# Seven edits to an FFT and expert-routing kernel: weight loads, a shorter load chain, one plain transform, a new order

## The chip, the cores and the metric

The kernel runs on one core of one Trainium2 chip. The metric is the device time of one execution in microseconds (us), lower is better; several runs are taken and the median is named.

## The reference

x has 8 batches of 2496 rows of 256 numbers. Each batch goes through a real FFT along its rows, a complex 256x256 product with bias, a soft shrinkage, and the inverse FFT. All 19968 rows are then routed to 8 experts: pairs of row and expert are taken in falling order of their logit, a row goes to the first expert that still has room, each expert takes 2496 rows, and its rows pass a two-layer network.

```python
X = np.fft.rfft(x, axis=1)
Yr = Xr @ w_r - Xi @ w_i + b_r
Yi = Xr @ w_i + Xi @ w_r + b_i
Yr = sign(Yr) * max(abs(Yr) - 0.01, 0)
Yi = sign(Yi) * max(abs(Yi) - 0.01, 0)
y = np.fft.irfft(Yr + 1j * Yi, n=2496, axis=1)
...
logits = y @ w_gate
for idx in argsort(-logits.flatten()):
    tok, e = idx // 8, idx % 8
    if assigned[tok] >= 0 or counts[e] >= 2496: continue
    assigned[tok] = e; counts[e] += 1
out[assigned == e] = max(y @ w1[e], 0) @ w2[e]
```

## The kernel before, in words

**Transforms (to about 525 us).** The FFT of length 2496 is done as products with fixed matrices. Per batch, eleven units of two column groups pass the first transform (L1158): the piece of x, `xt` of 117 rows by 512, is split into a rounded high part (ACT's cast, L1041) and the rest (DVE's subtraction, L1044), and three matmuls, high by high matrix, low by high matrix, high by low matrix, stand for one full-precision product. L1161 writes the result to DRAM and a second load brings it back turned. Batch 0 alone turns it on the core: PE transposes against an identity matrix (`h_idn`, built on GpSimd, called POOL in the profile) at L1175. The second stage (L1198) follows, then the spectral product with w_r and w_i (`wt`, L1214 and L1222), which takes its operands split too (L1203 to L1208), then the shrinkage: L1227 on DVE, and then for the batches in `SOFT` L1229 on ACT and L1230 on DVE, for the others L1232 and L1233 on DVE. The third stage is L1243; its result goes through DRAM to the last transform (L1280 split, or L1273 in one full-precision matmul for the batches in `PLAIN5`, which is batch 7), and the logits come at L1303.

**Head of the program.** All loads of constants, weights, bias and the first pieces of x are issued by SP (SyncE). `chain` ties them into one order: batch 0's x, the second-stage matrix in parts (`FX`, L1067), the spectral weights (L1087), the four copies of the gate's weights (L1096), the two bias rows, spread over 128 partitions (L1082), the third-stage matrix (`GX`, L1070), and only then batch 1's first piece of x (L1121).

**Routing and experts (from about 370 us).** Each expert's threshold is found by counting rounds (L468 to L514: DVE compares and counts, PE adds over partitions, L478 and L508). Once an expert is full, its rows' numbers are put into a list and the expert's remaining rows are worked off, which the code calls a closing; there are eight. 512-row jobs of rows that are certain run earlier. A job gathers its rows by indirect DMA on POOL (L664), stores and loads them in blocks on SP (L671, L675) and transposes them (L688), runs the first layer (L717) and the second (L736, L737) on PE, and scatters the result (L749, POOL).

**A closing's weights.** Which expert closes is known only as a number that the core computed. `load` fetches w1[e] and w2[e] in two halves each by indirect DMA on POOL (L641): an index tile `wi` holds the row number of each partition. Early jobs, whose expert is known, use plain DMA on SP (L639). Each half is split like the transforms' operands, by ACT's cast (L650) and DVE's subtraction (L651), 512 elements at a time, and frees its raw buffer then. For a closing's w1 the halves are read as `p (g k t) -> p g k t`, every fourth word.

**What sets the order.** Every instruction is added to a planner (class `Plan`) with an estimated duration, a due position, the buffers that it reads and writes, and an optional slack. `run` simulates the engines with these costs and emits the instruction that can start first, within a margin by due position; the emission order is each engine's program order. The positions come from a table `Q` and numbers such as `P1X`, `SLACK` and `LATE`; other numbers there give another order in every part of the program.

Of the kernel before, what the change touches and what calls it, by code (L numbers as in the profile page):

```python
# [13 lines left out]
I32 = mybir.dt.int32  # L14
# [266 lines left out]
P1X = -9.511  # L281
LATE = dict(sp=1.71, raw=7.61, gather=2.51, scatter=6.24)
SLACK = dict(split=1.565, count=0.366, back=0.155, lists=0.715, os=1.464, hid=0, mm4=0.149, mm4l=1.175, tr=1.717, trl=3.296, gate=1.037, gatel=2.447)
IOTA = True
Q = dict(hV=0.075, hA=0, hT=0, hP=0.003, e0=44.525, e1=79.699, en=128.427, le=5.378, ge=20.658, c0=1025.722, cs=57.378, c1=1077.172, c1a=1050.482, n0=126.722, n2=109.33, ll=59.361, gs=61.594, gl=3.592, be=14.408, bl=79.116, xp=17.05, f0=8.927, p1=0.211, p1s=0.613, p57=4.061, p57s=3.032, p5=4.568, p56s=0.773, p5s=0.966, xl=3.381, xs=1.132, m2=0.126, m3=-1.213, zz=1.738, m4=0.206, l5=4.727, s5=-1.32, w5=1.063, t5=1.684, g5=-0.333, r0=10.696, gb=0.7, gw=0.71, lg=0.568, aa=0.354, ba=1.906, sc=4.867, k2=2.422, xw=1.628, xv=4.067, xv2=4.926, gl2=11.503)
SOFT = (2, 3, 4, 5, 6)
# [172 lines left out]
def count(K, H, pos, c, no, ag, cols, pk, junk, acc, eqs=[], nt=1):  # L459
# [7 lines left out]
    for k in range(n):  # L467
        v(cols + 59, p, lambda k=k: V.scalar_tensor_tensor(junk[k % 2].t[:, 0:cols], H.m[:, 0:cols], c.t[:, k // ng:k // ng + 1], ag(k % ng)[:, 0:cols], op0=OP.is_ge, op1=OP.mult, accum_out=acc.t[:, k:k + 1]),  # L468
          [H.b_m, c, H.b_AG] + eqs, [junk[k % 2], acc])
# [76 lines left out]
def lists(K, H, pos, pre, ps2, cols, nt, iota, bs, pk, jl, gi, o, top, parts, group=None):  # L546
# [21 lines left out]
    for a, b in parts:  # L568
        for t0 in range(a, b, per):
# [9 lines left out]
            for q in range(n):  # L579
                plan.add('A', .29 + cols / 1200, pos(), lambda q=q, t=t0 + q, pl3=pl3: A.activation(K.junk.t[:, 0:cols], pl3.t[:, q, 0:cols], AF.Sign, bias=bs.t[:, t:t + 1], accum_out=sg.t[:, k0 + t:k0 + t + 1]), [pl3, bs], [sg, d], slack=SLACK['lists'])  # L580
# [38 lines left out]
class Experts:  # L619

    def __init__(self, K, H, YD, YDb, w1, w2, out):
        self.K, self.H, self.YD, self.YDb, self.out = K, H, YD, YDb, out
        self.w = (w1, w2)
        self.rows = (w1.rearrange("e d f -> (e d) f"), w2.rearrange("e (r m) d -> (e r) (m d)", m=4))
        self.scat = []

    def load(self, pos, e=None, wi=None, block=False):

        K, plan, v = self.K, self.K.plan, self.K.v
        W1, W2 = [], []  # L630
        for k in range(2):
            for m in range(2):
# [4 lines left out]
                if e is not None:  # L637
                    src = self.w[k][e].rearrange("(m p) f -> p m f", m=2)[:, m] if not k else self.w[k][e].rearrange("(g m p) d -> p g m d", g=2, m=4)[:, m]
                    K.dma(p, lambda r=r, src=src, k=k: K.nc.sync.dma_start(r.t.rearrange("p (m d) -> p m d", m=4) if k else r.t, src), 524e3, [], [r], run=1024 if k else 4096)  # L639
                else:  # L640
                    K.ind(p, lambda r=r, k=k, m=m: K.P.indirect_dma_start(out=r.t, out_offset=None, in_=self.rows[k],  # L641
                                                                          in_offset=bass.IndirectOffsetOnAxis(ap=wi.t[:, (2 + m if block and not k else m):(2 + m if block and not k else m) + 1], axis=0)), 524e3, [wi], [r], run=4096, late=LATE['raw'])
# [146 lines left out]
class Router:  # L789
# [10 lines left out]
    def early(self, pos):  # L800
# [11 lines left out]
        for e in range(8):  # L812
# [33 lines left out]
    def closing(self, i, pos):  # L846
# [117 lines left out]
        wa, wb, wi = K.sb("wi", [128, 1]), K.sb("wi", [128, 1]), K.sb("wi", [128, 4], I32)  # L964
        v(1, pw, lambda: V.tensor_scalar(wa.t, wf.t, 7.0, 256.0, op0=OP.min, op1=OP.mult), [wf], [wa])
        v(1, pw, lambda: V.tensor_tensor(wb.t, wa.t, H.pc[:, 1:2], op=OP.add), [wa, H.b_pc], [wb])
# [26 lines left out]
PLAIN1, PLAIN5 = (), (7,)  # L993
# [5 lines left out]
def phase_a(K, H, x, w_r, w_i, b_r, b_i, w_gate, cD1, cF, cG, cD5, YD, LG, NB=B):  # L999
# [51 lines left out]
    df = sb("xh", [117, 120])  # L1051
# [27 lines left out]
    def load_weights(after):  # L1079
        Bbt = sb("s2h", [128, 2, 256])  # L1080
        for c, bv in enumerate((b_r, b_i)):
            wl.append(add_dma(-79, lambda c=c, bv=bv: nc.sync.dma_start(Bbt.t[:, c], bass.AP(tensor=bv.tensor, offset=bv.offset, ap=[[0, 128], [1, 256]])), 128e3, [], [Bbt], late=0))  # L1082
# [13 lines left out]
        for q in range(4): wl.append(add_dma(-79, lambda q=q: nc.sync.dma_start(wg[32 * q:32 * q + 32, :, 8 * q:8 * q + 8], w_gate.rearrange("(m c) e -> c m e", c=32)), 8e3, [], [Bwg], after=[z_], run=32, late=0))  # L1096
# [5 lines left out]
    def batch(b):  # L1102
# [24 lines left out]
        for u in range(NU):  # L1127
# [23 lines left out]
            h, l = [sb(k, [117, 2, 256], F32R) for k in ("xh", "xl")]  # L1151
            ps = psum("p1", [120, 2, 256])
            st = gates['s1st', b, u] = sb("s1st", [120, 2, 256])
            split(pos1(u) - Q['xs'], t, lambda t=t, r=r, k_=k_: t.t[0:k_, r:r + 2], (h, lambda h=h, k_=k_: h.t[0:k_]), (l, lambda l=l, k_=k_: l.t[0:k_]), 'A', 'V', 512)

            def mm(h=h, l=l, ps=ps, k_=k_, M=M):
                for i, (a, v) in enumerate(((0, h), (0, l), (1, h))):
# [408 lines left out]
```

## Time and profile before

| what | value |
|---|---|
| median of 3 runs | 1454.51 us (1452.92 to 1456.67) |
| the profiled execution's own time | 1458.17 us |
| its span from first to last instruction | 1456.4 us |
| mean granted TensorE clock | 0.995 of full |
| PE (matmul) busy | 1422.1 us, 98% |
| PEld (weight load) busy | 1200.7 us, 82% |
| DVE busy | 1119.2 us, 77% |
| ACT busy | 813.3 us, 56% |
| POOL busy | 473.3 us, 32% |

PE is TensorE's matmul side and PEld its weight loads, which overlap matmuls; DVE is VectorE, ACT ScalarE, POOL GpSimd, SP the engine that issues plain DMAs. Matmuls are pipelined and their ends are modelled, so a PE shown busy need not be at its peak. Idle time of an engine that nothing waits for costs nothing.

### The profile page before, as it was taken

To read this page: it belongs to the slowest core of one execution; us is meant where nothing else is said; L and a number is where in the kernel's file an instruction comes from. 1 tells how busy PE (TensorE), PEld (TensorE's weight loads), DVE (VectorE), ACT (ScalarE), POOL (GpSimd) and SP (SyncE) were. 2 spreads that over 40 slices of the span, in tenths; PEclk is the share of its full clock that TensorE was granted. 3 is DMA by queue.
4 is the path that set the end of the run, shared out by engine and by line. 5 is a ranking of instruction groups with operands and counts; after the bars stand their busy time and mean duration, and the time that the engine had idled before them with its cause. 6 is when DMAs were issued, how large, how long until landed. Compare 5 with 4: busy or idle time off the path is not lost.

```text
span 1456.4 us, 33431 instructions
## 1 busy us (share of the span) xinstructions
PE 1422.1 (98%) x9630; PEld 1200.7 (82%) x9630; DVE 1119.2 (77%) x3210; ACT 813.3 (56%) x1919; POOL 473.3 (32%) x442
## 2 busy tenths in 40 slices
PE   8999999999999999999999999999999999999997
PEld 6978888888887867888888878788888888888886
DVE  4879778877999986899999999987876564553432
ACT  4766887878778765446536364545444652442331
POOL 0012222222224234312534454546354435312112
PEclk9999999999999999999999999999999999999999
DMA  6588797888877676332743545544443344321000
GB/s 209 170 289 273 222 299 224 284 277 242 269 212 264 200 202 210 125 115 83 208 116 113 162 123 156 154 139 135 131 143 121 99 136 139 110 71 37 24 23 30
DMA packets 218596, 238.11 MB, mean 163 GB/s; under 512 B 96310, under 2 KB 180387, under 8 KB 218403
## 3 DMA queue, kind: packets, MB, share of 16 engines
q1 hardware_dynamic: 198433, 177.56, 40.2%
q0 software_dynamic: 19840, 58.22, 12.8%
q8 instruction: 78, 1.28, 0.4%
q14 instruction: 115, 0.94, 0.2%
q10 hardware_dynamic: 130, 0.11, 0.0%
HBM read 138.10 MB, written 97.71 MB: 162 GB/s over the span
## 4 chain that ended last, share of the span: by engine, by line
PE 79%; DVE 13%; DMA 3%; ACT 2%; issue 2%; SPq 0%; POOL 0%; POOLq 0%; DVEq 0%; ACTq 0%
PE b L717 23%; PE b L736 15%; PE b L737 8%; PE b L1214 6%; PE b L1243 4%; PE b L1198 3%; PE pt L717 3%; PE b L1222 3%; PE b L1158 3%; PE pt L736 3%; PE b L1280 2%; PE pt L737 1%; PE b L1303 1%; DMA xt<-in_x_dram 1%; DVE xTl L1207 1%
## 5 line engine op out<-in xcount | busy, mean ns | idle before, releaser
L1044 POOL TENSOR_TENSOR s2l<-s2c,s2h 120x512 fp32r<-120x512 f32 (+1 forms) x84 | 107.4, 1289 | 396.5 <-ACT s2h L1041 336.5
L1214 PE MATMUL b<-wt,xTh 128*128 128x256 f32 x640 | 125.1, 291 | 0.0
L749 POOL DMA_INDIRECT out_dram<-xTh,li x64 | 66.4, 1038 | 171.4 <-DVE xTh L746 112.8
L1214 PEld LDWEIGHTS b<-wt,xTh 128*128 128x128 f32 x640 | 100.4, 191 | 9.6 <-issue 3.6
L1214 PE MATMUL b<-wt,xTl 128*128 128x256 f32 x320 | 93.8, 293 | 6.0 <-DVE xTl L1207 5.7
L749 POOL DMA_INDIRECT out_dram<-xTl,li x64 | 67.3, 1051 | 95.6 <-DVE xTl L746 53.8
L1198 PEld LDWEIGHTS b<-FG,sh 128*128 128x128 f32 x640 | 85.4, 194 | 9.3 <-issue 2.3
L1198 PE MATMUL b<-FG,sh 128*128 128x128 f32 x640 | 91.3, 280 | 1.2 <-DVE sh L1179 1.2
L1243 PE MATMUL b<-y,FG 64*128 64x256 f32 x640 | 81.2, 390 | 0.5 <-DVE y L1233 0.5
L745 ACT COPY xTh<-b 128x256 f32<-128x256 f32 x61 | 22.8, 374 | 86.1 <-PE b L737 85.3
L1243 PEld LDWEIGHTS b<-y,FG 64*128 64x128 f32 x640 | 58.6, 186 | 14.8 <-issue 2.6
L1214 PEld LDWEIGHTS b<-wt,xTl 128*128 128x128 f32 x320 | 61.2, 191 | 11.4 <-DVE xTl L1207 10.6
L1158 PE MATMUL b<-xh,d 117*120 117x512 f32 (+1 forms) x154 | 64.3, 424 | 5.4 <-ACT xh L1041 5.4
L1293 DVE STREAM_TRANSPOSE yT<-b 128x512 f32<-128x512 f32 x87 | 61.5, 709 | 8.3 <-PE b L1273 4.5
L1044 DVE TENSOR_TENSOR xl<-xt,xh 117x512 fp32r<-117x512 f32 (+1 forms) x77 | 53.9, 707 | 16.6 <-ACT xh L1041 16.1
L1280 PE MATMUL b<-s2h,d 120*128 120x512 f32 (+1 forms) x168 | 66.4, 404 | 0.0
L1227 DVE TENSOR_TENSOR y<-b,sx 128x512 f32<-128x512 f32 x80 | 54.8, 685 | 15.0 <-ACT sx L1225 14.0
L1216 DVE TENSOR_TENSOR b<-b,bf 128x512 f32<-128x512 f32 x80 | 55.3, 692 | 12.5 <-PE b L1214 12.5
L580 ACT ACTIVATE ajunk<-b,h_bs 128x156 bf16<-128x156 f32 x122 | 47.7, 391 | 27.5 <-PE b L575 23.1
L1282 ACT COPY yst<-b 117x512 f32<-117x512 f32 (+2 forms) x95 | 52.2, 557 | 19.4 <-DVE yT L1293 12.6
L1222 PE MATMUL b<-wt,xTh 128*128 128x256 f32 x320 | 62.9, 288 | 0.0
L717 PE MATMUL b<-yT,sh 128*128 128x512 f32 (+1 forms) x170 | 61.3, 384 | 0.0
(1154 smaller groups left out, 4947.0 us busy)
## 6 DMA issues: line engine op xcount, KB each, us to landing
T<-s4st SPq DMA_DIRECT2D x80, 256.0 KB
s2c<-T SPq DMA_DIRECT2D x80, 240.0 KB
YD<-yst SPq DMA_DIRECT2D x80, 234.0 KB
xt<-in_x_dram SPq DMA_DIRECT2D x35, 512.0 KB
sh<-T SPq DMA_DIRECT2D x35, 512.0 KB
T<-s1st SPq DMA_DIRECT2D x70, 240.0 KB
xt<-in_moe_w_dram SPq DMA_DIRECT2D x32, 512.0 KB
yT<-XG SPq DMA_DIRECT2D x48, 64.0 KB
```

What stands on the lines that cost most here:

```text
L717: T.matmul(ps.t[:, 0:w], lhsT=W1[m].t[:, a, 128 * ft:128 * ft + 128], rhs=x_.t[:, 0:w], start=q + m == 0, stop=q + m == 3)
L736: T.matmul(ps.t, lhsT=hh.t[:, u:u + 128], rhs=W2[ft // 4].t[:, :, ft % 4], start=ft == 0, stop=False)
L737: T.matmul(ps.t[:, 0], lhsT=hl.t[:, u:u + 128], rhs=w_[0], start=False, stop=ft == 7)
L749: ins = P.indirect_dma_start(out=self.out, out_offset=bass.IndirectOffsetOnAxis(ap=oi.t[0:M, oo + t:oo + t + 1], axis=0), in_=o.t[0:M], in ...
L1044: lambda: eng.tensor_tensor(lb[1](), src(), hb[1](), op=OP.subtract), [srcb, hb[0]], [lb[0]], port=True)
L1158: T.matmul(ps.t[0:M], lhsT=d1[0:k_, a, 0:M], rhs=v.t[0:k_], start=i == 0, stop=i == 2)
L1198: T.matmul(ps.t[:, :, dt, i], lhsT=sh[k // 8].t[:, k % 8, 128 * dt:128 * dt + 128], rhs=at(Ft, k), start=True, stop=True)
L1214: T.matmul(pc.t[:, c], lhsT=a.t[:, 1 - c, dt], rhs=wt[2 - c].t[:, w, dt], start=dt == 0 and a is th and w == 0, stop=dt == 1 and a is tl)
L1222: T.matmul(pa.t, lhsT=a.t[:, 2, dt], rhs=wt[0].t[:, w, dt], start=dt == 0 and a is th and w == 0, stop=dt == 1 and a is tl)
L1243: T.matmul(ps4[i].t[:, r], lhsT=at(Gt, 2 * (p - 1 + r) + c)[h], rhs=zs[r].t[h, c], start=c == 0, stop=c == 1)
L1280: T.matmul(ps.t[:, gs_], lhsT=d5[0:k_, a], rhs=v.t[0:k_, gs_], start=i == 0, stop=i == 2)
L1293: yt.append(plan.add('V', TU, pos + Q['t5'], lambda yT=yT, ps=ps: V.transpose(yT.t.rearrange("p g m r -> p (g m r)"), ps.t.rearrange("p g ...
```

## The change

Seven edits, with the lines of the kernel after some ten higher:

1. A closing's second weights come by plain DMA from SP; its address is made from a register that SP loads from a new element of `wi` (written by one more DVE operation). The first weights stay with POOL's indirect DMA.
2. The first weights' halves are now read as straight runs of 512.
3. The two bias copies and the four gate copies are issued by POOL and are no longer part of SP's chain.
4. Batch 6's first transform is one full-precision matmul per unit, without the split; its matrix `df` gets a tile of its own (`d1f`).
5. Batch 7 joins `SOFT`.
6. The planner's costs of counting, scan, list and sign steps and of the third stage are changed.
7. `P1X`, `SLACK` and `Q` hold new numbers throughout.

```diff
@@ constants
-P1X = -9.511
+P1X = -8.849
...
-SOFT = (2, 3, 4, 5, 6)
+SOFT = (2, 3, 4, 5, 6, 7)
+PLAIN1, PLAIN5 = (6,), (7,)
...
@@ counting
-        v(cols + 59, p, lambda k=k: V.scalar_tensor_tensor(junk[k % 2].t[:, 0:cols], ...
+        v(155 + cols, p, lambda k=k: V.scalar_tensor_tensor(junk[k % 2].t[:, 0:cols], ...
...
@@ lists
-            v(2 * C, pos(), lambda gm=gm, pre=pre: V.tensor_tensor_scan(...
-            v(65 + C, pos(), lambda gm=gm, pre=pre, mk=mk, lim=lim: V.scalar_tensor_tensor(...
+            v(4.5 * C, pos(), lambda gm=gm, pre=pre: V.tensor_tensor_scan(...
+            v(225 + C, pos(), lambda gm=gm, pre=pre, mk=mk, lim=lim: V.scalar_tensor_tensor(...
...
@@ load (weights of a closing)
+                elif k:
+                    def ld(r=r, m=m, reg=reg):
+                        if not m: reg.append(K.nc.values_load(wi.t[0:1, 4:5], engines=[mybir.EngineType.SP], ...))
+                        K.nc.sync.dma_start(r.t.rearrange("p (m d) -> p m d", m=4), self.w[1][bass.ds(reg[0], 1)].rearrange("o (g m p) d -> p (o g) m d", g=2, m=4)[:, m])
+                    q = K.dma(p, ld, 524e3, [wi], [r], run=1024)
+                    if m: q.ords.add(last)
+                    last = q
                 else:
-                    K.ind(p, lambda r=r, k=k, m=m: K.P.indirect_dma_start(out=r.t, out_offset=None, in_=self.rows[k],
...
+                    c = (2 if block else 0) + m
+                    K.ind(p, lambda r=r, c=c: K.P.indirect_dma_start(out=r.t, out_offset=None, in_=self.rows, ...
...
-                    return (W.t[:, i - 1].rearrange("p (g t k) -> p g t k", g=2, t=4) if i else r.t.rearrange("p (g k t) -> p g t k" if e is None else "p (g t k) -> p g t k", g=2, t=4))[:, o]
+                    return (W.t[:, i - 1] if i else r.t)[:, 512 * o:512 * o + 512]
...
@@ load_weights
-            wl.append(add_dma(-79, lambda c=c, bv=bv: nc.sync.dma_start(Bbt.t[:, c], ...), 128e3, [], [Bbt], late=0))
+            add_dma(-60, lambda c=c, bv=bv: nc.gpsimd.dma_start(Bbt.t[:, c], ...), 128e3, [], [Bbt], 'P', late=0)
...
-        for q in range(4): wl.append(add_dma(-79, lambda q=q: nc.sync.dma_start(wg[32 * q:32 * q + 32, :, 8 * q:8 * q + 8], ...
+        for q in range(4): add_dma(-50, lambda q=q: nc.gpsimd.dma_start(wg[32 * q:32 * q + 32, :, 8 * q:8 * q + 8], ...
...
-            chain(head + FX[0:1] + wl[2:4] + wl[4:] + FX[1:2] + wl[0:2] + FX[2:3] + GX[0:1] + FX[3:] + GX[1:])
+            chain(head + FX[0:1] + wl + FX[1:3] + GX[0:1] + FX[3:] + GX[1:])
...
@@ first transform
+            if b in PLAIN1:
+                plan.add('T', .86, pos1(u), lambda t=t, r=r, ps=ps, k_=k_, M=M: T.matmul(ps.t[0:M], lhsT=df.t[0:k_, 0:M], rhs=t.t[0:k_, r:r + 2], start=True, stop=True), [t, df], [ps])
...
@@ a closing's index tile
-            g8, wf, wi = sb("g8", [128, 8]), sb("wi", [128, 1]), sb("wi", [128, 2], I32)
+            g8, wf, wi = sb("g8", [128, 8]), sb("wi", [128, 1]), sb("wi", [128, 8], I32)
+            v(1, pos(), lambda wf=wf, wi=wi: V.tensor_scalar(wi.t[:, 4:5], wf.t, 7.0, 0.0, op0=OP.min, op1=OP.max), [wf], [wi])
```

The order of instructions moves at three places that matter here.

**The head, on SP.** Before, from the spectral weights to batch 1's first piece of x (`FG` holds matrix parts, `s2h` the bias, `wg` the gate's weights):

```order
7 L1087 DMA y_171<-in_w_i_dram 128x2x256
8 L1096 DMA wg<-in_moe_w_gate_dram 32x8x8 x4
9 L1067 DMA FG_164<-cF 128x768
10 L1082 DMA s2h_183<-in_b_r_dram 128x256
11 L1082 DMA s2h_183<-in_b_i_dram 128x256
12 L1067 DMA FG_164<-cF 128x768
13 L1070 DMA FG_192<-cG 128x1024
14 L1067 DMA FG_194<-cF 128x512
15 L1070 DMA FG_192<-cG 128x1024
16 L1070 DMA FG_208<-cG 128x512
17 L1072 DMA yT_215<-cD 120x256
18 L1121 DMA xt_267<-in_x_dram 128x1024
```

and in the changed kernel, first SP and then POOL, which had the identity matrix (`h_idn`) as its first work:

```order
7 L1096 DMA y_173<-in_w_i_dram 128x2x256
8 L1076 DMA FG_165<-cF 128x768 x2
9 L1079 DMA FG_182<-cG 128x1024
10 L1076 DMA FG_184<-cF 128x512
11 L1079 DMA FG_182<-cG 128x1024
12 L1079 DMA FG_188<-cG 128x512
13 L1081 DMA yT_190<-cD 120x256
14 L1130 DMA xt_268<-in_x_dram 128x1024
```

```order
5 L1576 UNCONDITIONAL_BRANCH
6 L1091 DMA s2h_116<-in_b_r_dram 128x256
7 L1091 DMA s2h_116<-in_b_i_dram 128x256
8 L1105 DMA wg<-in_moe_w_gate_dram 32x8x8 x4
9 masks.py:197 MEMSET h_idn 128x128
10 masks.py:199 ISA
11 masks.py:199 AFFINE_SELECT h_idn<-h_idn 128x128
```

SP's row of the piece of x moves up by the six copies; POOL's identity now stands behind them.

**A closing's second weights, POOL and SP.** Before, POOL fetches them (`xt`, L641) among gathers (L664), with spacers between (L349):

```order
244 L664 DMA xl_11377<-YD,li_10583 128x256
245 L349 ISA x14
246 L641 DMA xt_11456<-in_moe_w_dram,wi_10301 128x1024
247 L349 ISA x14
248 L641 DMA xt_11489<-in_moe_w_dram,wi_10301 128x1024
```

In the changed kernel SP does, between its stores (`XG`, L680) and loads (L684) of blocks:

```order
539 L680 DMA XG_11149<-s2c_10883 128x2x256
540 L684 DMA ex_11300<-XG_11149 32x8x64 x4
541 L680 DMA XG_11390<-FG_11210 128x2x256
542 L644 TENSOR_LOAD wi_10260
543 L645 ISA
544 L645 DMA xt_11419<-in_moe_w_dram 128x4x256
545 L645 ISA
546 L645 DMA xt_11440<-in_moe_w_dram 128x4x256
547 L680 DMA XG_11468<-s4st_11284 128x2x256
548 L684 DMA s2c_11520<-XG_11390 32x8x64 x4
549 L680 DMA XG_11627<-xl_11403 128x2x256
550 L684 DMA FG_11634<-XG_11468 32x8x64 x4
```

The two loads of the second weights have left POOL and stand, behind a register load, ahead of three block loads (L684) on SP's queue.

**Batch 6's first transform, on PE.** Before, each unit has three matmuls of L1158:

```order
1484 L1198 MATMUL b_4519<-FG_164,sh_4340 128x2x64 x4
1485 L1158 MATMUL b_4531<-xh_4206,d_95 120x512
1486 L1158 MATMUL b_4531<-xl_4263,d_95 120x512
1487 L1158 MATMUL b_4531<-xh_4206,d_95 120x512
1488 L1280 MATMUL b_4540<-s2h_4452,d_96 128x512
```

and in the changed kernel one, straight from the piece of x:

```order
1390 L1211 MATMUL b_4303<-FG_184,sh_3490 128x2x64 x4
1391 L1293 MATMUL b_4318<-s2h_4261,d_96 128x512
1392 L1293 MATMUL b_4318<-s2l_4272,d_96 128x512
1393 L1293 MATMUL b_4318<-s2h_4261,d_96 128x512
1394 L1166 MATMUL b_4328<-xt_4115,d1f 120x512
1395 L1316 MATMUL b_4341<-yT_4052,wg 32x64
```

Eleven such units change from three matmuls to one.

## Rows read from the trace of the kernel before

**Rows 1.** Busy time by stretch: us, engines' busy us (x instructions), PE clock, DMA share, GB/s:

```profile
85.00:370.00 285.00, 282.36 (x2608) 247.30 (x2606) 228.70 (x403) 222.80 (x488) 68.17 (x53) 0.99 0.83 259
370.00:525.00 155.00, 145.85 (x1468) 123.89 (x1468) 150.11 (x420) 114.94 (x290) 48.34 (x41) 1.00 0.74 235
525.00:1075.00 550.00, 545.65 (x3086) 446.28 (x3085) 491.64 (x1771) 276.03 (x695) 236.81 (x225) 1.00 0.49 144
```

**Rows 2.** PE's waits: what waited, for whom, us in total, times, longest:

```profile
PE b L1214 <- DVE xTl L1207: 5.7, 10, 1.4
...
PE b L508 <- DVE ge L506: 3.4, 4, 1.0
```

**Rows 3.** Timeline of PE in the head: start us, us, what [idle before <-releaser]:

```profile
16.52 1.76 PE L1175 MATMUL b<-h_idn,sp 128*128 128x128 f32 x12 [0.55 <-DVE sp L1146]
...
24.00 0.28 PE L1214 MATMUL b<-wt,xTl 128*128 128x256 f32 x1
27.91 0.78 PE L1158 MATMUL b<-xh,d 117*120 117x512 f32 x1 [3.63 <-ACT xh L1041]
```

**Rows 4.** Timeline of ACT in the head:

```profile
27.24 1.14 ACT L1041 CAST xh<-xt 117x512 fp32r<-117x512 f32 x2 [4.52 <-DMA xt<-in_x_dram]
```

**Rows 5.** Busy time in stretches of 2 us, columns as in rows 1:

```profile
10.00:12.00 2.00, 2.00 (x20) 2.00 (x20) 0.79 (x3) 0.90 (x6) 0.00 (x0) 1.00 1.04 392
...
14.00:16.00 2.00, 1.97 (x18) 1.82 (x17) 1.75 (x5) 1.41 (x6) 0.00 (x0) 1.00 0.76 181
16.00:18.00 2.00, 1.43 (x11) 1.27 (x12) 1.66 (x6) 1.49 (x6) 0.00 (x0) 1.00 0.91 110
28.00:30.00 2.00, 2.00 (x4) 1.29 (x5) 2.00 (x4) 2.00 (x5) 0.00 (x0) 0.50 0.00 0
34.00:36.00 2.00, 2.00 (x17) 2.00 (x17) 1.23 (x3) 0.37 (x1) 0.00 (x0) 0.89 0.00 1
```

**Rows 6.** Timeline of SP's queue in the head, columns as in rows 3:

```profile
6.17 4.58 SPq L1096 DMA_DIRECT2D wg<-in_moe_w_gate_dram  x4
...
12.46 0.35 SPq L1082 DMA_DIRECT2D s2h<-in_b_r_dram  x1
...
17.83 0.53 SPq L1121 DMA_DIRECT2D xt<-in_x_dram  x1
```

**Rows 7.** The chain of work that ended last: start us, us, what:

```profile
27.91 3.22 PE b L1158 x6
...
55.97 1.40 PE b L1158 x6
...
539.43 1.79 PE b L1273 x4
```

**Rows 8.** Groups of ACT by form: out<-in xcount | busy us, mean ns | idle before:

```profile
L1041 ACT CAST xh<-xt 117x512 fp32r<-117x512 f32 x70 | 42.8, 626 | 5.3 <-DMA xt<-in_x_dram 5.2
...
L1229 ACT ACTIVATE y<-y,ml 128x512 f32<-128x512 f32 x50 | 36.2, 725 | 12.2 <-DVE y L1227 11.3 <-DVE g L527 0.5
```

**Rows 9.** Groups of DVE by form, columns as in rows 8:

```profile
L1044 DVE TENSOR_TENSOR xl<-xt,xh 117x512 fp32r<-117x512 f32 x70 | 49.2, 711 | 16.5 <-ACT xh L1041 16.1
...
L1232 DVE TENSOR_SCALAR y<-y 128x512 f32<-128x512 f32 x30 | 13.3, 442 | 0.3
```

**Rows 10.** Line L651, 695 to 1290 us: ns min/median/max; who waited (us, times):

```profile
L651 DVE TENSOR_TENSOR FG<-xt,FG x20: 674/682/722, 701.7 to 1287.8; 128x512 fp32r<-128x512 f32 x20
L651 DVE TENSOR_TENSOR sp<-xt,sp x16: 1045/1069/1090, 719.3 to 1183.2; 128x512 fp32r<-128x512 f32 x16
...
  POOL xt L641: 36.7, 6
```

**Rows 11.** Line L1532, near the program's end: a register load on SP's queue:

```profile
L1532 SPq TENSOR_LOAD <-h_fail x1: 492/492/492, 1331.0 to 1331.0; - x1
```

**Rows 12.** Timelines of SP and DVE around a closing's block: load issued, first use:

```profile
739.49 2.06 SPq L675 DMA_DIRECT2D xl<-XG  x4
...
743.95 0.44 DVE L688 STREAM_TRANSPOSE y<-yT 128x256 f32<-128x256 f32 x1
```

More of the change, by code (lines that the diff above doesn't have):

```diff
@@ L623, in __init__ @@
         self.w = (w1, w2)
-        self.rows = (w1.rearrange("e d f -> (e d) f"), w2.rearrange("e (r m) d -> (e r) (m d)", m=4))
+        self.rows = w1.rearrange("e d f -> (e d) f")
         self.scat = []
@@ L639, in load @@
                     K.dma(p, lambda r=r, src=src, k=k: K.nc.sync.dma_start(r.t.rearrange("p (m d) -> p m d", m=4) if k else r.t, src), 524e3, [], [r], run=1024 if k else 4096)
-                else:
-                    K.ind(p, lambda r=r, k=k, m=m: K.P.indirect_dma_start(out=r.t, out_offset=None, in_=self.rows[k],
-                                                                          in_offset=bass.IndirectOffsetOnAxis(ap=wi.t[:, (2 + m if block and not k else m):(2 + m if block and not k else m) + 1], axis=0)), 524e3, [wi], [r], run=4096, late=LATE['raw'])
+                elif k:
+                    def ld(r=r, m=m, reg=reg):
+                        if not m: reg.append(K.nc.values_load(wi.t[0:1, 4:5], engines=[mybir.EngineType.SP], min_val=0, max_val=7, skip_runtime_bounds_check_because="the number of an expert, held to at most 7 where it is written"))
+                        K.nc.sync.dma_start(r.t.rearrange("p (m d) -> p m d", m=4), self.w[1][bass.ds(reg[0], 1)].rearrange("o (g m p) d -> p (o g) m d", g=2, m=4)[:, m])
+                    q = K.dma(p, ld, 524e3, [wi], [r], run=1024)
+                    if m: q.ords.add(last)
+                    last = q
+                else:
+                    c = (2 if block else 0) + m
+                    K.ind(p, lambda r=r, c=c: K.P.indirect_dma_start(out=r.t, out_offset=None, in_=self.rows, in_offset=bass.IndirectOffsetOnAxis(ap=wi.t[:, c:c + 1], axis=0)), 524e3, [wi], [r], run=4096, late=LATE['raw'])
                 def part(i, o, k=k, r=r, W=W):
                     if k: return W.t[:, i - 1, 2 * o:2 * o + 2] if i else r.t.rearrange("p (m d) -> p m d", m=4)[:, 2 * o:2 * o + 2]
-                    return (W.t[:, i - 1].rearrange("p (g t k) -> p g t k", g=2, t=4) if i else r.t.rearrange("p (g k t) -> p g t k" if e is None else "p (g t k) -> p g t k", g=2, t=4))[:, o]
+                    return (W.t[:, i - 1] if i else r.t)[:, 512 * o:512 * o + 512]
                 for o in range(2):
@@ L1050, in phase_a @@
     add_dma(-100, lambda: A.dma_start(ds.t, cD1.rearrange("p (h m) -> p h m", h=2)), 112e3, [], [ds], 'A', run=960, k=13, late=0)
-    df = sb("xh", [117, 120])
+    df = K.one("d1f", [117, 120])
     plan.add('V', dve(120), -90, lambda: V.tensor_tensor(df.t, ds.t[:, 0], ds.t[:, 1], op=OP.add), [ds], [df])
@@ L1095, in load_weights @@
         z_ = plan.add('V', dve(256), -14, lambda: V.memset(wg, 0.0), [], [Bwg])
-        for q in range(4): wl.append(add_dma(-79, lambda q=q: nc.sync.dma_start(wg[32 * q:32 * q + 32, :, 8 * q:8 * q + 8], w_gate.rearrange("(m c) e -> c m e", c=32)), 8e3, [], [Bwg], after=[z_], run=32, late=0))
+        for q in range(4): add_dma(-50, lambda q=q: nc.gpsimd.dma_start(wg[32 * q:32 * q + 32, :, 8 * q:8 * q + 8], w_gate.rearrange("(m c) e -> c m e", c=32)), 8e3, [], [Bwg], 'P', after=[z_], run=32, late=0)
     CHUNKS = [(0, 2), (2, 4), (6, 4), (10, 4), (14, 4), (18, 4)], [(0, 4), (4, 4), (8, 4), (12, 4), (16, 4), (20, 2)]
@@ L1244, in batch @@
             gates['mm4', b, p] = [0]
-            gates['mm4', b, p][0] = plan.add('T', 2.12, pos + Q['m4'], mm4, zs + zd + [BG_[part(GQ, 2 * p)]], list(ps4), uses=[Gt[p // 8]], slack=SLACK['mm4l' if b == NB - 1 else 'mm4'])
+            gates['mm4', b, p][0] = plan.add('T', 1.95, pos + Q['m4'], mm4, zs + zd + [BG_[part(GQ, 2 * p)]], list(ps4), uses=[Gt[p // 8]], slack=SLACK['mm4l' if b == NB - 1 else 'mm4'])
             for i in range(2):
```

35 lines of the change are left out of this document (18 added, 17 removed).

## Prediction, made before the changed kernel had run

> **What bounds the kernel now.** I read the busy time by stage first, then the list of TensorE's waits, then the first 36 us in order of time. The windows [rows 1] show that TensorE (PE) is the engine that runs out of room in most of the program. From 525 to 1075 us, the early expert jobs and most routing rounds, it is busy 545.65 of 550 us; from 85 to 370 us, the transforms alone, 282.36 of 285 us. A busy PE is not a PE at its peak, so these are upper ends, but in those stretches only VectorE (DVE) comes near, with 491.64 us in the first of the two. From 370 to 525 us, where the last transforms and the first routing run together, DVE is the fullest: 150.11 of 155 us, while PE is down to 145.85. So a saving counts on PE everywhere, on DVE between 370 and 525 us, and elsewhere only where PE waits.
>
> The waits [rows 2] are few: matmuls of the spectral product on L1207 5.7 us, of the routing rounds on L506 3.4 us. The longest single one is of another line, in the head. PE's last matmul of batch 0's product starts at 24.00 us and the next, the first transform of batch 1, at 27.91 after 3.63 us of waiting [rows 3]; the cast on ScalarE (ACT) that it waits for had itself waited 4.52 us for its piece of x [rows 4], which SP issued only at 17.83 us [rows 6]. What follows is dearer than it looks: after that idle stretch the granted clock is 0.50, the lower of the two levels, at 28 to 30 us, and in the window from 34 it is still 0.89 [rows 5].
>
> **Early small loads to GpSimd's queue.** Two bias copies and four gate copies leave SP's chain. The gate's four alone occupy SP for 4.58 us from 6.17 [rows 6]. Their bytes do not vanish, and the DMA engines were not free: in the 4 us from 14 to 18 us, after the first bias copy went out at 12.46 [rows 6], they show a busy share of 0.76 and 0.91 while moving 181 and 110 GB/s, against 392 GB/s at 10 to 12 us [rows 5]. Lower end of what the piece of x gains: the idle share, 2 x (1 - 0.76) + 2 x (1 - 0.91) = 0.66 us. Upper end: those 4 us moved 582 KB, which at 392 GB/s takes 1.5 us, a gain of 2.5 us; and SP is no longer held either, which could give back the full 3.63 us of PE's wait. With the wait the low clock may go. Six matmuls of L1158 take 3.22 us at 27.91, and 1.40 us at full clock [rows 7]; the stretch from 28 to about 34 us is some 6 us at half clock, worth 3 us at most, less what DVE's chain would hold back anyway. So the head gives 0.7 to 6.6 us. I take 4.5, nearer the upper end, since the slow windows moved under half of what the engines can, and an early issue lets the slow packets share the engines with large ones: 2.4 us of the wait, and 2.1 for the clock. The identity matrix is now built on GpSimd behind the six copies; the transposes that use it come at 16.52 us [rows 3], and at the 4.58 / 4 = 1.15 us a copy that the gate's cost on SP it is ready by some 8 us, so I cost that at nothing.
>
> The Trainium skill has a rule against this edit ("DMA: Bandwidth & Descriptors", Issuing engines are not separate DMA queues): copies started from several engines end on the same 16 DMA engines, and only the time to initiate them is saved. By it the head would give about 0.7 us; the busy shares of 0.76 and 0.91 [rows 5] speak for it, the 4.58 us of issue [rows 6] against it.
>
> **Batch 6's first transform plain.** Each of 11 units loses one ACT cast (0.626 us [rows 8]) and one DVE subtraction (0.711 us [rows 9]): 6.9 us of ACT, 7.8 of DVE. PE gets one full-precision matmul for three: the last transform of batch 7 already runs so, and four such matmuls take 1.79 us, which is two units at 0.895 each, against 1.40 / 2 = 0.70 for a unit of three split ones [rows 7]. (The four records are the two passes of two units.) That is 11 x 0.195 = 2.1 us more on PE, before 525 us, where PE is 94 to 99% busy. The relief can only win back PE's waits on DVE there, at most some 2.0 of the 5.7 us. Between +2.1 and -2.0 I take 0.
>
> **Batch 7's shrinkage.** In ten pieces DVE loses the 0.442 us of L1232 [rows 9] (the operation behind it gives way to one of like kind and size), 4.4 us where DVE is full. ACT gets 0.725 us for each [rows 8], 7.3 us, and has 114.94 of 155 us taken [rows 1]. Against it, each piece's chain grows by 0.725 - 0.442 = 0.28 us, 3 us in ten. Between -4.4 and +3 I take -2.
>
> **Closing weights.** Plain rows of the first weights let the split read in a straight line. DVE's halves are 0.68 us where they read straight and 1.07 where they read every fourth word [rows 10]: 4 x 0.39 us a closing, 12 us in eight. PE is 99% busy beside it, so by itself this is worth nothing but margin for the routing rounds. GpSimd loses 16 loads and their spacers; SP gets 16 loads and eight register loads of 0.49 us [rows 11]. The loads move the same bytes in pieces of 1 KB instead of 4; the DMA engines' share there is 0.49 [rows 1], which leaves room. One more tiny operation a closing on DVE is under 0.44 us each. I cost all this at nothing; the cover is the lead that SP has with the blocks, and what happens without it is a rival below.
>
> **New plan.** The planner's cost of counting, scan and list steps is raised, and all constants of the order are new. What it can win is the 3.4 us of L506 waits [rows 2] and parts of the others; it can also put a matmul ahead of its input somewhere new, and I allow it as much as the waits of L1207 that it has to avoid again, less what is left of them: +4. I take -1, between -3.4 and +4.
>
> **Sum.** -4.5 + 0 - 2 + 0 - 1 = -7.5 us against this execution's own 1458.17 us (span 1456.4, 1.8 around it): 1450.7. The execution lies 3.7 above the median of 1454.51, so on the median **1447.0**. With every term at its best the sum is -16.4, at its worst +8.4: 1438 to 1463.
>
> **Rivals.**
> - *The DMA engines are the limit of the head.* Busy shares of 0.76 to 1.04 [rows 5] speak for it. x comes 0.66 us earlier, the 0.50 clock stays: -0.7 - 2 - 1 = -3.7, **1450.8**, at the edge of what can be measured. By the skill's rule on issuing engines this is the outcome. Chance 0.20.
> - *Batch 0 pays.* The bias copies now run beside batch 0's x. If the 2.5 us that they cost at 14 to 18 us move to the first microseconds, PE's first transforms start that much later and the head wins nothing: +2.5 - 2 - 1, about **1454**, no difference. Chance 0.10.
> - *SP is blocked by the second weights.* GpSimd waited 36.7 us in six waits for the split to free a raw buffer [rows 10], 6.1 us each. If such waits are now SP's, the gathered blocks' copies queue behind them; a block's load was issued 4.5 us ahead of its first use (739.49 to 743.95 [rows 12]). Where SP's wait exceeds 4.5 us the transposes come late, and with 1.6 us in each of eight closings PE loses 13 us: 1447 + 13 = **1460**. Against it: raw buffers come free sooner with the faster split. Chance 0.10.
> - *The plan closes the gaps too.* Head 6.6, shrinkage 4.4, L506 3.4, batch 6 2.0: -16.4, **1438.1**. Chance 0.12.
>
> **Chances.** The forecast's own case has 0.48 and reaches from 1441 to 1452. A measurement can tell about 0.3%, 4.4 us, from no change: faster is under 1450.1, slower over 1458.9. Faster: 0.43 of the forecast, 0.09 of the first rival, all 0.12 of the last, 0.64. Slower: the blocked SP and 0.02 of the batch 0 case, 0.12. The rest, 0.24, is no difference. The range 1438 to 1456 leaves out the blocked SP and the far tails of the others.
>
> **What would show it.** Right: SP issues batch 1's first piece of x well before 17.8 us; its cast waits under 2 us; the clock stays 1.00 from 24 to 36 us; the end of batch 0's and 1's work comes 4 to 5 us earlier. Batch 6's units show matmuls of about 0.45 us in pairs and no cast; PE's busy time before 525 us rises by about 2 us. Splits on DVE all read near 0.68 us. Wrong: x landing as late as before, or a 0.50 clock after it (first rival); gaps between PE's first matmuls of batch 0 (second); SP waiting on L651's successor while PE waits for the ffn's inputs (third). If the head gains as said and the end does not, the loss lies in the new order, and the stage where the shift shrinks names it.

## The result, and the profile after

The changed kernel takes 1439.99 us (median of 4 runs, 1439.27 to 1440.78), the kernel before 1453.78 (4 runs, 1452.92 to 1456.67): a ratio of **0.9901** on record, 95% interval 0.9887 to 0.9914, so 14.4 us less (12.5 to 16.4; the two medians alone differ by 13.8). The forecast was 1447.0, 7.5 us less than the 1454.51 known then: the right sign, about half the size, inside the range of 1438 to 1456 but outside the forecast's own case of 1441 to 1452.

The execution of the changed kernel that was profiled took 1440.23 us, about its median; the one of before took 1458.17, 4.4 us over this section's median. So of the 18 us between the two spans (1456.4 and 1438.4) some 4 are no effect of the change. Counted by PE's matmuls of the experts' first layer (1920 in each kernel), the 120th starts at 592.0 us before and 581.0 after, the 1120th at 1078.9 and 1062.6: 11.0 us of the 18 lie ahead of the 120th, 5.2 between the two and 1.7 behind.

Busy time by stretch, in the columns of [rows 1]:

```profile
85.00:370.00 285.00, 282.62 (x2601) 245.87 (x2601) 225.70 (x397) 215.92 (x477) 66.59 (x53) 0.99 0.82 258
370.00:525.00 155.00, 152.17 (x1556) 130.28 (x1554) 147.58 (x424) 126.70 (x319) 52.58 (x46) 1.00 0.78 248
525.00:1075.00 550.00, 549.66 (x3082) 452.08 (x3082) 488.74 (x1827) 268.90 (x688) 228.20 (x219) 1.00 0.49 143
```

PE's idle time fell from 9.15 to 2.83 us between 370 and 525 us, and from 4.35 to 0.34 between 525 and 1075; from 85 to 370 us it is as it was (2.64 and 2.38). These are stretches of time, and by the last of them the changed kernel is some 11 us further on in its program; counted from the 120th to the 1120th matmul, PE's idle time is 4.35 us before and 0.00 after. PE's waits, in the columns of [rows 2]:

```profile
PE b L1227 <- DVE xTl L1220: 3.0, 6, 0.7
PE b L1211 <- DMA sh<-T: 2.4, 1, 2.4
PE b L1146 <- DMA sh<-in_x_dram: 1.4, 1, 1.4
```

The spectral product's waits on VectorE (5.7 us on what was L1207) are 3.0, the routing rounds' 3.4 us on L506 are gone from the list, and two waits for DMAs are new; one of them, L1146, is batch 0's first transform waiting for x.

The head, in the timelines of PE, ACT and SP (columns as in [rows 3]). PE:

```profile
9.81 7.65 PE L1146 MATMUL b<-d1f,sh 117*128 117x120 f32 x64 [1.43 <-DMA sh<-in_x_dram]
18.24 1.76 PE L1188 MATMUL b<-h_idn,sp 128*128 128x128 f32 x12 [0.78 <-DVE sp L1155]
...
26.64 0.49 PE L1171 MATMUL b<-xh,d 117*120 117x512 f32 x1 [0.64 <-ACT xh L1050]
```

ACT:

```profile
25.97 1.14 ACT L1050 CAST xh<-xt 117x512 fp32r<-117x512 f32 x2 [1.80 <-DMA xt<-in_x_dram]
```

SP:

```profile
16.63 0.35 SPq L1130 DMA_DIRECT2D xt<-in_x_dram  x1
```

and the clock, in windows, first one of the kernel before and then two of the changed kernel:

```profile
30.00:40.00 10.00, 9.99 (x66) 9.51 (x65) 6.83 (x14) 5.41 (x13) 0.00 (x0) 0.78 0.20 51
```

```profile
28.00:30.00 2.00, 2.00 (x15) 1.84 (x14) 1.85 (x4) 2.00 (x6) 0.00 (x0) 1.00 0.00 0
30.00:40.00 10.00, 9.66 (x83) 9.19 (x83) 9.32 (x20) 4.54 (x12) 0.00 (x0) 1.00 0.18 51
```

Batch 0's transposes come 1.7 us later than before (18.24 against 16.52 in [rows 3]), batch 1's first transform only 1.3 us earlier (26.64 against 27.91). But PE's idle stretch ahead of it is 0.64 us instead of 3.63, and the granted clock stays at 1.00 where it was 0.50 from 28 to 30 us [rows 5] and 0.78 from 30 to 40.

### The profile page after: what moved, and what is told of

The parts are those of the page before. It is cut to its first block, busy times and chain, and to the rows that moved or that the text cites. A ratio compares the mean times of both kernels' runs of the same rounds, so it can differ in the third digit from the quotient of the medians.

```text
span 1438.4 us, 33189 instructions
## 1 busy us (share of the span) xinstructions
PE 1414.4 (98%) x9619; PEld 1195.2 (83%) x9619; DVE 1090.1 (76%) x3197; ACT 799.2 (56%) x1918; POOL 457.5 (32%) x432
## 3 DMA queue, kind: packets, MB, share of 16 engines
q1 hardware_dynamic: 205505, 185.65, 42.3%
## 4 chain that ended last, share of the span: by engine, by line
PE 89%; DVE 4%; DMA 3%; ACT 2%; issue 1%; SPq 0%; POOL 0%; POOLq 0%; DVEq 0%; ACTq 0%
PE b L726 27%; PE b L745 17%; PE b L746 8%; PE b L1227 7%; PE b L1256 4%; PE b L1211 4%; PE pt L726 4%; PE b L1235 3%; PE pt L745 3%; PE b L1293 3%; PE b L1171 2%; PE pt L746 2%; PE b L1316 1%; PE b L748 1%; DMA xt<-in_x_dram 1%
## 5 line engine op out<-in xcount | busy, mean ns | idle before, releaser
L754 ACT COPY xTl<-b 128x256 f32<-128x256 f32 x69 | 25.8, 374 | 78.4 <-PE b L746 69.7
L755 DVE TENSOR_TENSOR xTl<-b,xTl 128x256 f32<-128x256 f32 x69 | 28.9, 419 | 46.7 <-ACT xTl L754 46.6
L1295 ACT COPY yst<-b 117x512 f32<-117x512 f32 (+1 forms) x93 | 51.4, 562 | 17.2 <-DVE yT L1306 8.1
L1053 DVE TENSOR_TENSOR xl<-xt,xh 117x512 fp32r<-117x512 f32 (+1 forms) x66 | 49.6, 763 | 12.5 <-ACT xh L1050 9.5
```

What stands on the lines that cost most here:

```text
L1053: lambda: eng.tensor_tensor(lb[1](), src(), hb[1](), op=OP.subtract), [srcb, hb[0]], [lb[0]], port=True)
```

## The experiments

Each part was added to the kernel before by itself, and taken out of the changed kernel by itself. The runs were made in groups. The kernel before took 1454 us beside the runs of the first two parts, the first three with a moved due position and the one under "Relief or order", and 1458 to 1459 beside the others, so only ratios to the kernel before are compared. A thousandth is 1.45 us; each ratio's interval is some 1 to 1.5 thousandths either way, so a difference between two ratios is known to about 2 to 3 us.

| part | alone in the kernel before | taken out of the changed kernel (0.9901) |
|---|---|---|
| new numbers | 1.0015 (1.0006 to 1.0023) | 0.9922 (0.9911 to 0.9934) |
| batch 7 in SOFT | 1.0020 (1.0010 to 1.0029) | 0.9914 (0.9901 to 0.9927) |
| batch 6 plain | 0.9960 (0.9945 to 0.9976) | 0.9907 (0.9891 to 0.9923) |
| these three together | 0.9953 (0.9939 to 0.9967) | not run |
| small loads on GpSimd | 0.9990 (0.9981 to 0.9999) | 0.9916 (0.9901 to 0.9931) |
| closings' weights | 0.9953 (0.9940 to 0.9966) | 0.9950 (0.9937 to 0.9964) |

### The new numbers

```diff
-P1X = -9.511
+P1X = -8.849
...
-        v(cols + 59, p, lambda k=k: ...
+        v(155 + cols, p, lambda k=k: ...
```

(and `SLACK`, `Q` and the other costs; the second run has the reverse edit in the changed kernel)

> The kernel before with the change's numbers alone: P1X, SLACK, Q and the planner's costs. Theory A (the new order itself brings what came beyond the head): 6 to 10 us off, about 1446, most of it gained between 370 and 1075 us, with the waits of L508 on L506 (3.4 us before) gone. Theory B (the relief of VectorE by batch 7's shrinkage and batch 6's plain transform brings it, and the numbers only fit the order to that): within 2 us of before, about 1454, since the work on VectorE between 370 and 525 us is as before.

> The changed kernel with the old numbers (P1X, SLACK, Q, costs). Theory A: 6 to 10 us slower than the changed kernel, 1446 to 1450. Theory B: 0 to 3 us slower, 1440 to 1443.

Alone the numbers make the kernel before 2.2 us slower, against theory A and just outside theory B's 2 us; without them the changed kernel loses 3.1 us, less than theory A said, about theory B's upper end. The new order is not where the gain comes from, though it fits the changed kernel better than the old one. In the run with old numbers the 120th to the 1120th matmul of the first layer (counted in PE's timeline) take 480.7 us, in the changed kernel 481.6 and in the kernel before 486.8: the gain of the expert part is there without the new numbers.

### Batch 7's shrinkage

```diff
-SOFT = (2, 3, 4, 5, 6, 7)
+SOFT = (2, 3, 4, 5, 6)
```

(in the changed kernel; the other run has the reverse edit in the kernel before)

> The changed kernel with batch 7's shrinkage as before (SOFT without 7). Theory B: 4 to 9 us slower than the changed kernel, 1444 to 1449, lost between 370 and 525 us where VectorE is then full again. Theory A: at most 2 us slower, 1440 to 1442.

> The kernel before with batch 7 in SOFT alone. Theory B: 3 to 8 us off, 1446 to 1451. Theory A: within 2 us of before, 1452 to 1456. The prediction's own term was -2 us.

1.9 us lost in the changed kernel, with an interval that overlaps that kernel's own, and 2.9 us slower when added alone. Theory B fails in both; the second result lies a little outside theory A's 2 us too.

### The small loads

```diff
-            add_dma(-60, lambda c=c, bv=bv: nc.gpsimd.dma_start(...), ..., 'P', late=0)
+            wl.append(add_dma(-79, lambda c=c, bv=bv: nc.sync.dma_start(...), ..., late=0))
...
-            chain(head + FX[0:1] + wl + FX[1:3] + GX[0:1] + FX[3:] + GX[1:])
+            chain(head + FX[0:1] + wl[2:4] + wl[4:] + FX[1:2] + wl[0:2] + FX[2:3] + GX[0:1] + FX[3:] + GX[1:])
```

(and the gate's copies; the other run has the reverse edit in the kernel before)

> The kernel before with the bias and gate copies on GpSimd's queue and the shorter chain alone. Theory C (the head brings about 3.5 us, by the granted clock that stays up from 20 to 40 us): 3 to 5 us off, about 1450, clock 1.00 from 28 to 36 us although batch 0's first matmuls come some 1.5 us later. Theory D (the first transforms after the head absorb it, since they wait for DVE and DMA anyway): within 1.5 us of before.

> The changed kernel with the six small loads back in SP's chain. Theory C: 3 to 5 us slower than the changed kernel, 1443 to 1445, with the 0.50 clock back at 28 to 30 us. Theory D: within 1.5 us of it.

1.5 us gained in one direction, 2.2 lost in the other. The clock does what theory C says: windows of the changed kernel with the loads back on SP show the 0.50 again,

```profile
28.00:30.00 2.00, 2.00 (x5) 1.22 (x6) 2.00 (x4) 2.00 (x6) 0.00 (x0) 0.50 0.00 0
30.00:40.00 10.00, 9.66 (x70) 9.25 (x69) 7.16 (x15) 5.27 (x13) 0.00 (x0) 0.87 0.19 51
```

and its last transposes of batch 0 start at 46.5 us against 43.6 in the changed kernel. In the medians less than that 2.9 us is left of it: 1.5 us is theory D's edge, 2.2 lies between the two theories.

Two things make this part easier to read in the traces than in the medians. PE's order of instructions is the same with and without this edit, in both kernels, so no new order is mixed into it. And the run with the loads back on SP can be set beside the two other variants of the changed kernel run with it (the next section's first two, which keep the new head and PE's order as far as this): its 120th matmul of the first layer starts at 589.6 us, theirs at 585.5 and 585.9. In these single executions 3.7 to 4.1 us of the head's gain are still there when the expert part begins.

### The closings' weights

First the straight read alone is taken back: the first weights' split reads every fourth word again (`p (g k t) -> p g t k`; the words on `load` ahead of the prediction have the last two letters exchanged). To fit that, the second weights' loads on SP fetch four neighbouring rows per partition, in pieces of 4 KB instead of 1. In the two traces the compute engines run the same instructions in the same order as in the changed kernel.

```diff
-K.nc.sync.dma_start(r.t.rearrange("p (m d) -> p m d", m=4), self.w[1][bass.ds(reg[0], 1)].rearrange("o (g m p) d -> p (o g) m d", g=2, m=4)[:, m])
+K.nc.sync.dma_start(r.t, self.w[1][bass.ds(reg[0], 1)].rearrange("o (g p m) d -> p (o g) (m d)", g=2, m=4)[:, m])
...
-                    return (W.t[:, i - 1] if i else r.t)[:, 512 * o:512 * o + 512]
+                    return (W.t[:, i - 1].rearrange("p (g t k) -> p g t k", g=2, t=4) if i else r.t.rearrange("p (g k t) -> p g t k" if e is None else ...))[:, o]
```

> The changed kernel with the second weights still by plain DMA on SP, but laid out as before (four rows to a partition), so that the first weights' split reads every fourth word again; the order of instructions on every engine is the same. Theory E (the straight split brings the gain of the expert part, 6 to 8 us from 590 to 1080 us): 5 to 8 us slower than the changed kernel, 1445 to 1448, with waits of the routing rounds' matmuls on VectorE back. Theory F (taking the second weights off GpSimd brings it): within 2 us, 1439 to 1442. The prediction's term for both was nothing.

0.9934 (0.9920 to 0.9947), 4.8 us more than the changed kernel. Line L660 is the split's subtraction; in the changed kernel its groups read (columns as in [rows 10])

```profile
L660 DVE TENSOR_TENSOR sp<-xt,sp x32: 646/684/830, 438.5 to 1164.9; 128x512 fp32r<-128x512 f32 x32
...
  POOL xt L651: 2.8, 2
```

and in the run with the strided read

```profile
L660 DVE TENSOR_TENSOR sp<-xt,sp x32: 640/935/1093, 440.3 to 1174.7; 128x512 fp32r<-128x512 f32 x32
```

(the last line is the same there; half of the 32 belong to early jobs and read straight in both runs, the closings' 16 take 1.05 to 1.09 us), with these waits of PE from 525 to 1100 us, and this window:

```profile
PE b L509 <- DVE ge L507: 2.3, 4, 0.9
PE b L1286 <- DMA s2c<-T: 1.6, 1, 1.6
```

```profile
525.00:1075.00 550.00, 545.88 (x3046) 446.83 (x3045) 489.88 (x1813) 275.18 (x682) 228.09 (x218) 1.00 0.48 143
```

Of the 3.4 us that the routing rounds waited in [rows 2], 2.3 are back (on L509, which is L508 of the kernel before), and PE's idle time is 4.1 us again where the changed kernel has 0.34. L1286's wait for a transform's load is not the split's: two other runs that keep the straight read and PE's order (the loads back on SP, and the loads held back, below) have 1.3 us on it. Since PE's order is unchanged, each of its instructions can be compared with itself: from 560 us to 1009 us this run falls behind the changed kernel by 3.7 us more; 3.3 of that come in five steps of 0.4 to 1.0 us, all at a matmul of L509, between 714 and 988 us. The stretch from the 120th to the 1120th matmul takes 485.2 us instead of 481.6. So with the same program order and one slower read on ACT and DVE the routing rounds' chain is late again: theory E, a little under its lower end of 5 us. That the larger pieces of the second weights have a part in this is not excluded by a run of its own, but L509 waits for DVE, and GpSimd's waits for raw buffers are the same 2.8 us. Which of the two engines' relief counts, DVE's or ACT's, was not separated.

Then all of the closings' part, taken out and added alone (the diff is the one shown ahead of the prediction, under `load`):

> The changed kernel with the closings' weights as before: second ones by indirect DMA on GpSimd, strided split. Theories E and F: 6 to 9 us slower, 1446 to 1449. If the prediction's zero was right: within 2 us.

> The kernel before with the closings' weights alone as in the change (second weights by plain DMA on SP, straight split). Theory E (the straight split takes VectorE and ScalarE time out of the routing rounds, whatever the order): 4 to 8 us off, ratio 0.9945 to 0.997, and the stretch from the 120th to the 1120th matmul of the first layer, 486.8 us before, comes to 481 to 483. Theory G (it pays only with the new order): ratio over 0.998.

7.1 us lost, 6.8 us gained: the one part that gives the same in both directions, the largest of all. The stretch from the 120th to the 1120th matmul takes 481.1 us in the kernel before with this part alone, and 486.1 in the changed kernel without it. Over all twenty kernels of this document it takes 480.5 to 481.6 us in the nine that read the first weights straight and 485.2 to 486.8 in the eleven that do not, whatever their numbers, `SOFT`, batch 6, small loads or due position: a new order is no rival for these 5 us. Of the 7.1 us the straight read has 4.8; for the other 2.3 the intervals of the two runs overlap, and that they come from the second weights' way by SP is not shown. GpSimd's wait for a raw buffer, 36.7 us in [rows 10], is 2.8 in both runs above.

That wait did not vanish. It is SP's now, as the rival with the blocked SP had it. SP's queue in the changed kernel, 695 to 1300 us (what waited, for whom, us in total, times, longest):

```profile
SPq L645 <- DVE sp L660: 26.8, 5, 18.9
...
SPq L645 <- DVE sh L660: 15.5, 1, 15.5
```

That is 42.3 us in six waits for the split to free a raw buffer, two of them far over the 4.5 us from which the rival counted a loss. Its premise came, its price did not: the list of PE's waits between 695 and 1300 us of the changed kernel is empty. The register loads cost 0.27 us each. What covers the waits was not tried.

### Batch 6's plain transform, and the three together

```diff
-PLAIN1, PLAIN5 = (), (7,)
+PLAIN1, PLAIN5 = (6,), (7,)
```

(in the kernel before, with the new branch and the matrix's own tile; then the reverse in the changed kernel; then this with SOFT and the new numbers in the kernel before)

> The kernel before with batch 6's first transform plain alone. Theory H (PE pays 2 us and the relief is hidden, the prediction's term): between 2 us off and 2 us on, ratio 0.9985 to 1.0015. Theory I (the relief of ScalarE and VectorE lets the transforms run ahead): 3 to 6 us off, ratio 0.996 to 0.998.

> The changed kernel with batch 6's first transform split again. Theory H: ratio to the kernel before 0.989 to 0.9915 (the changed kernel's own is 0.9901). Theory I: 0.993 to 0.995.

> The kernel before with the new numbers, batch 6 plain and batch 7 in SOFT, so all of the change but the small loads and the closings' weights. Theory J (these three fit each other: alone the numbers and SOFT each cost 2 us, together they give 4 to 6 us between the end of batch 6 and the first jobs): ratio 0.996 to 0.9975. Theory K (the parts add up, and the gain is the closings' weights and the head): ratio over 0.999.

Alone the plain transform gives 5.8 us (theory I), taken out it costs 0.9 (theory H). The three together give 6.8 us, though two of them cost time alone: theory J, a little over its upper end. PE's own price was forecast rightly; two records are one unit, 0.86 us in the chain (0.895 was taken):

```profile
308.44 0.86 PE b L1166 x2
```

### What another order does

Most edits above also make another order, since the planner starts from new costs and dependencies (the strided read makes none, and the small loads none on PE). To see what that alone does, one due position was moved by a tenth.

```diff
-Q = dict(..., p1=0.211, ...)
+Q = dict(..., p1=0.311, ...)
```

(0.111 in the second run; 0.31 and 0.11 in place of 0.21 in the changed kernel)

> The kernel before with the due position of the first transforms of batches 2 to 7 moved from 0.211 to 0.311, nothing else: the planner makes another order. Theory L (orders differ by luck, as much as the single parts of the change do): ratio off 1 by 0.002 or more in at least one of this run and the next. Theory M (the order matters little): both within 0.0015 of 1.

> The same, moved to 0.111. Theories L and M as for the other shift.

> The changed kernel with the same due position moved from 0.21 to 0.31. Theory N (its numbers are the best of many orders, so another one loses): ratio to before 0.992 to 0.995 against the changed kernel's 0.9901. Theory M: 0.989 to 0.9915.

> The changed kernel with the due position of the first transforms moved from 0.21 to 0.11. Theory N (numbers that are the best of many orders): ratio to before 0.992 to 0.996. Theory M: 0.989 to 0.9915.

| | 0.1 later | 0.1 earlier |
|---|---|---|
| kernel before | 1.0015 (1.0006 to 1.0024) | 0.9978 (0.9970 to 0.9987) |
| changed kernel (0.9901) | 0.9946 (0.9933 to 0.9959) | 0.9930 (0.9917 to 0.9944) |

The kernel before gets 2.2 us slower by the one and 3.2 us faster by the other, the changed kernel slower by both, 6.5 and 4.2 us. So theory L holds, and theory N (with two neighbours each, no more). Then a part that moves the time by 2 or 3 us through the planner can't be told from a new order by one run, which holds for SOFT and for the numbers; and the changed kernel's own order is better than both of its neighbours by as much as a whole part of the change.

### Relief or order, for the plain transform

The kernel before with batch 6's matmul plain, but its casts and subtractions still made and their results unused:

```diff
-            if b not in PLAIN1: h, l = [sb(k, [117, 2, 256], F32R) for k in ("xh", "xl")]
+            h, l = [sb(k, [117, 2, 256], F32R) for k in ("xh", "xl")]
...
-            if b not in PLAIN1: split(pos1(u) - Q['xs'], t, ...
+            split(pos1(u) - Q['xs'], t, ...
```

> The kernel before with batch 6's first transform as one full-precision matmul, but with the 11 casts on ScalarE and 11 subtractions on VectorE still made, their results unused. With the split left out the ratio was 0.996. Theory I (relief of ScalarE and VectorE is the gain): back to 0.999 to 1.002. Theory O (the gain is not the relief, but PE no longer waiting for the split, or the order): 0.995 to 0.998.

0.9984 (0.9974 to 0.9993), between what the two theories allow, and nearer to 1 than the 0.9960. Some 3.5 us of the 5.8 go with the relief of ACT and DVE, if the order has no part in it; by the scatter above it may have as much. This stays open.

### Small loads held back

The changed kernel with a tiny GpSimd copy, which needs the fifth of batch 0's pieces of x, ahead of the six small loads:

```diff
+        gt = plan.add('P', .1, -61, lambda: P.tensor_copy(Bbt.t[:, 0, 0:2], gate.t[:, 0, 0:2]), [gate], [Bbt])
...
-            ..., 128e3, [], [Bbt], 'P', late=0)
+            ..., 128e3, [], [Bbt], 'P', after=[gt], late=0)
```

> The changed kernel with one tiny GpSimd copy ahead of the six small loads that needs the fifth piece of batch 0's x, so that they start only when it is in. Theory P (the small loads took batch 0's DMA time): the last turn of batch 0's first half comes about 1.5 us earlier than in the changed kernel, and the end 1 to 2 us earlier, ratio 0.988 to 0.9895. Theory Q (batch 0 is late for another reason, or batch 1's piece of x gets later by as much): 0.9895 to 0.992.

0.9909 (0.9894 to 0.9924), the changed kernel's own time. Its head, PE and then ACT and SP:

```profile
15.54 1.76 PE L1189 MATMUL b<-h_idn,sp 128*128 128x128 f32 x12 [0.55 <-DVE sp L1156]
...
25.73 0.49 PE L1172 MATMUL b<-xh,d 117*120 117x512 f32 x1 [2.43 <-ACT xh L1050]
```

```profile
25.05 1.14 ACT L1050 CAST xh<-xt 117x512 fp32r<-117x512 f32 x2 [4.00 <-DMA xt<-in_x_dram]
```

```profile
13.69 0.35 SPq L1131 DMA_DIRECT2D xt<-in_x_dram  x1
```

Batch 0's transposes come at 15.54 us, 2.7 us before those of the changed kernel: the small loads had taken that from batch 0, as theory P says of the cause. But batch 1's piece of x, issued 2.9 us earlier (13.69 against 16.63), is cast only 0.9 us earlier (25.05 against 25.97), and what batch 0 won becomes for the most part PE's wait of 2.43 us. The ratio lies in theory Q's range; its interval just reaches P's. Compared instruction by instruction, in the same PE order, this run is 1.2 us ahead of the changed kernel from 95 to 377 us, and behind it after 560 us (on this see the last section), so what holding the loads back is worth stays open within some 2 us. The granted clock stays 1.00 from 28 to 40 us after this wait; after the 3.63 us of before it was 0.50.

## Why the prediction was right and wrong

**What bounds the kernel** was read rightly, and then not used. The windows [rows 1] showed 4.35 us of PE's idle time from 525 to 1075 us and the list [rows 2] put 3.4 of it on VectorE's L506. The prediction offered that sum to the new plan alone, and then took only 1 us of it.

**Closing weights: the step that failed.** "PE is 99% busy beside it, so by itself this is worth nothing but margin for the routing rounds." This term of the sum, put at nothing, measured 7 us in both directions, 4.8 of them with the straight read alone in an unchanged order. The margin was the gain: the strided halves stand on ACT and DVE among the rounds' operations, and most of the remaining PE idle time was the rounds waiting for DVE. A share of 99% over 550 us still holds 4.35 us of idle time; the list had named the engine that caused most of it, and the time that DVE would be rid of (12 us) was worked out in the same text. What ACT would be rid of was not: its casts of the closings' halves in the kernel before (16 of this row's 32 are of closings, the others of early jobs, which read straight; the closings' other 16 are on the tile `sh`)

```profile
L650 ACT CAST sp<-xt x32: 612/880/1159, 434.5 to 1180.3; 128x512 fp32r<-128x512 f32 x32
```

take 1.11 to 1.16 us where they read every fourth word and 0.62 where they read straight, 16 us more in eight closings.

**The head.** -4.5 was taken, 1.5 to 2.2 measured in the medians, 3.7 to 4.1 in single traces as far as the expert part. The clock came as described. The wait went mostly another way: 1.7 us of it is batch 0 being later (the second rival's mechanism, with 1.4 us of PE's waiting for x on L1146 as its sign), and the piece of x came 1.3 us earlier, not 2.4. By the rule of the Trainium skill ("DMA: Bandwidth & Descriptors", Issuing engines are not separate DMA queues) only the time to issue is saved. The held-back loads agree that more was not to be had from the queue: with an issue 2.9 us earlier the cast comes 0.9 us earlier. What the first rival did not have is that the lost clock still came back: by an estimate from the windows of before it was 2 x 0.50 + 10 x 0.22 = 3.2 us from 28 to 40 us, and it is nothing now, with PE's wait at 0.64 us.

**Batch 6, shrinkage, plan.** 0, -2 and -1 were taken, together -3; together they measured 6.8 us. PE's added cost was right to 0.04 us a unit. That the stretch from 370 to 525 us would gain was right as a whole, PE's idle time there fell from 9.15 to 2.83 us; that VectorE's relief did it is argued, not shown, and none of the three can be priced by itself. SOFT alone costs 2.9 us and the numbers alone 2.2, each about as much as one moved due position moves the time. The allowance for a new order, -3.4 to +4, had the right width for that scatter; putting the likeliest value near zero took no account that the changed kernel's numbers may be chosen among many orders, and two neighbouring ones lose 6.5 and 4.2 us.

By the table the groups add up to about the whole: closings 7, the head 1.5 to 2.2, the other three 6.8, some 15 to 16 against 14.4 measured. Without the closings that is 8.3 to 9.0 us, close to the 7.5 forecast, but with a smaller head and larger other parts: that these errors offset each other was luck. So was it that the range held the result; it reached that far by the best cases of the other terms. The last rival, 1438.1, came nearest, and PE's 3.4 us on L506 did go as it said, but by the closings' split and not by the plan.

## What to carry to other kernels

Where an engine is 98 or 99% busy, count its idle time in microseconds and by releaser before costing an off-path saving at nothing: the last few microseconds may nearly all wait for the engine that the edit relieves. Where a planner makes the order, price an edit in both directions and beside a neutral change of the order, and trust what agrees in both. Loads moved to another queue compete at once with whatever is loading then: look at what that is, and at which idle stretch gets shorter.

## What had not been expected of the hardware

The same DVE subtraction of 128 x 512 numbers takes 0.68 us from straight rows and up to 1.09 from every fourth word, ACT's cast 0.62 and up to 1.16. The first was in the prediction; that the read of one tile, with the order of instructions unchanged, is worth some 4 to 5 us of a kernel whose PE is 99% busy beside it was not. The Trainium skill ("SBUF — State Buffer", Door 1: The DMA port swizzle) says that consecutive accesses are at full rate only with two or more hits in a line of 16 bytes; every fourth word of four bytes has one, and the rows agree. A PE wait of 2.43 us was followed by a granted clock of 1.00, waits of 3.63 and (with the loads back on SP) 4.39 us by 0.50. The kernel before took 1454 us in some groups of runs and 1459 in others, 0.3%, as much as single parts of this change. Three traces from groups of the second kind have PE's order of the changed kernel (the strided read, the loads back on SP, the loads held back); against the changed kernel's own trace each falls 2.8 to 4.3 us behind between 461 and 559 us of that trace, where batch 7's last transforms stand and PE waits 1.3 to 1.6 us for one load (L1286; 0.3 us in the changed kernel's own trace). What differs there was not tried.
